# A static schedule rebuilt on measured ScalarE constants, and a GpSimd normalisation placed in halves beside VectorE's PSUM reads

## The chip, the cores and the metric

The kernel runs on one core of one Trainium2 chip. The metric is the device time of one execution in microseconds (us), median of several. The profiled execution of each kernel is one of those; its span, from first to last instruction, is about 2 us shorter than its time.

## The reference, cut to what matters

```python
x  = A_x                                   # 2048 tokens of 512, bf16
xn = layernorm(x)
# 32 heads of width 16; the scores are 32 x 2048 x 2048
o  = softmax(q @ k.T * 0.25) @ v           # q, k, v from xn @ wqkv
return x + o @ wo + (silu(xn @ w1) * (xn @ w3)) @ w2      # hidden width 1792
```

The exponentials are the bulk: 1024 tiles of 128x1024 scores. Most go through ScalarE's table; the rest are built on VectorE from integer operations on the bits of bf16 numbers.

Of the kernel before, what the change touches and what calls it, by code (L numbers as in the profile page):

```python
# [142 lines left out]

_LAT = 0.06
_LATS = {("pe", "act"): 0.041, ("pe", "dve"): 0.053, ("dve", "pool"): 0.083, ("pool", "dve"): 0.033, ("act", "dve"): 0.033}
_TAILS = {"act": 0.182, "dve": 0.083, "pool": 0.05, "sp": 0.0}


class _Sched(_Prog):
# [25 lines left out]
    def _time(self, op, deps, dur, tail, mode=None, rows=None):  # L175
        ready = self._ready(op, deps)
        if op.eng != "pe":
            start = max(self.free[op.eng], ready)
            op.end = start + dur + tail
            self.free[op.eng] = start + dur  # L180
            return op
        lm, lr, ls = self.pem
        if mode == "row":
            if lm == "row":
                gap = 0.217 if rows & lr else 0.007
            else:
                gap = 0.318
            start = max(ready, ls + gap)
            self.pem = (mode, rows | lr if gap < 0.1 and start < ls + 0.2 else rows, start)
            self.free["pe"] = start + 0.01  # L190
        elif mode == "col":
            start = max(ready, ls + (0.217 if lm == "col" else 0.318))
            self.pem = (mode, frozenset(), start)
            self.free["pe"] = start + 0.2
        else:
            start = max(ready, ls + (0.217 if lm == "x" else 0.318))
            self.pem = (mode, frozenset(), start + dur - 0.217)
            self.free["pe"] = start + dur
        op.end = start + dur + tail
        return op  # L200
# [836 lines left out]
def _plan_fast(nc, ps, flag, A_x, A_wqkv, A_wo, B_w1, B_w3, B_w2, out):  # L1037
# [49 lines left out]
    with ctx:  # L1087
# [65 lines left out]
        def xk(s0, n):  # L1153
            return [("xnT", t) for t in range(s0 // 128, (s0 + n) // 128)]

        a_cost = lambda n: 0.049 + 0.000834 * n
        d_cost = lambda n: 0.054 + 0.00106 * n
        s_cost = lambda n: 0.075 + 0.000261 * n

# [416 lines left out]
        def tile_OUT(tg, part):  # L1576
            qc, ts = divmod(tg, 4)

            def og(g, slot, key):
                return (lambda i: onorm[:, slot, ts * 128 + 32 * i:ts * 128 + 32 * i + 32], wo[:, g, :],  # L1580
                        [("ON", slot), ("wor", g)],
                        lambda: have(key))
            ffn = [(lambda i, fc=fc: hT[:, fc, ts * 128 + 32 * i:ts * 128 + 32 * i + 32], w2[:, fc, :],
                    [("hT", fc), ("w2", fc)], None) for fc in range(FC)]
# [61 lines left out]
            return _T("O%d_%d" % (tg, part), groups, evac, cond=cond, start=None if part in (2, 4) else start)  # L1646


        st = {"dbl": 0, "pos": 0, "pv": 0, "dbal": 0, "nd": 0, "lastA": -1.0, "n_exp": 0, "wait_a": 0, "hold_d": 0, "last_par": 0}
        pbuf = [0.0] * 3  # L1650
        pr_free = [0.0] * NPR
        yfree = [0.0] * NY
# [222 lines left out]
        def try_d():  # L1875
            if st["pos"] >= NR or st["early"] or st["hold_d"] or not d_due():
                return False
            free = open_bufs()
            if not free or (len(free) == 1 and st["wait_a"] == 0):
                return False  # L1880
            nx = d_next()
            buf = free[-1]
            b0 = 2 * buf
            x = score(b0, "D", *nx) if nx is not None else None
            if x is None:
                return False
            st["hold_d"] = 1
            u, j0, kt, o = x
            st["dbal"] += 1 - j0
            nd_unit[u] += 1  # L1890
            for i in range(2):
                ndj[u][j0 + i] += 1
            pbuf[buf] = 1e9
            sl = dcur[0]
            if sl is None:
                sl = dcur[0] = {"y": None, "p1": 0, "n": 0, "ch": [], "done": 0, "max": 2 if u < NU - 1 or left[u] > D_ONE else 1}
            c = sl["n"]
            sl["n"] += 1
            last = sl["n"] == sl["max"]
            if last:  # L1900
                dcur[0] = None
            sl["ch"].append((u, j0, kt))

            def p1():
                if sl["y"] is None:
                    sl["y"] = free_slot(yfree)
                    yfree[sl["y"]] = 1e9
                ys = sl["y"]
                q = P.op("dve", lambda e: e.tensor_scalar(dsl[:, ys, 1024 * c:1024 * c + 1024], ps[:, b0 * 512:b0 * 512 + 1024],  # L1909
                                                          YB, G_LO, ALU.add, ALU.max),  # L1910
                         reads=[("ps", b0), ("ps", b0 + 1)], writes=[("ds", ys, 2 * c), ("ds", ys, 2 * c + 1)] + xd_keys(ys, 1024 * c, 1024 * c + 1024), dur=d_cost(1024), name="p1")
                pbuf[buf] = q.end + _LAT
                st["hold_d"] = 0
                sl["p1"] += 1
                if last:
                    chain(sl)
            prev = dprev[0] if c == 0 else sl["prev"]
            if c == 0:
                sl["prev"] = prev
                dprev[0] = sl  # L1920
            need = 1 if c == 0 else 2
            P.post("dve", p1, ready=o.end + _LAT, prio=2,
                   cond=lambda: (sl["y"] is not None or free_slot(yfree) is not None) and
                   (prev is None or prev["done"] >= need))
            return True
# [113 lines left out]
        def unit_end(u, o):  # L2039
# [33 lines left out]
            def e4():  # L2073
# [3 lines left out]
                        reads=[("Rrow",)], writes=[("R", j, h)], kb=32)  # L2077
                if h or u == NU - 2:
                    eng = "dve" if u == NU - 2 else "pool"
                    P.post(eng, lambda: e5(eng), ready=q.end + _LAT, prio=0, cond=lambda: u // 2 < NON or all(  # L2080
                        ("OUT", (u // 2 - NON) // NP * 4 + i) in done for i in range(4)))

            def e5(eng):
                on = (u // 2) % NON
                if u == NU - 2:
                    q = P.op(eng, lambda e: e.scalar_tensor_tensor(onorm[:, on, :], U[:, 0, :], msk[:, 0:1], R[:, :],
                                                                   ALU.mult, ALU.mult),
                             reads=[("Uc",), ("msk", 0)] + [("R", j_, h_) for j_ in range(4) for h_ in range(2)],
                             writes=[("ON", on)], dur=0.68)
                    done[("ON", qc, pi)] = q.end + _LAT  # L2090
                    return
                q = P.op(eng, lambda e: e.tensor_tensor(onorm[:, on, :], U[:, 0, :], R[:, :], ALU.mult),  # L2092
                         reads=[("Uc",)] + [("Uo", j_) for j_ in range(4)] +
                         [("R", j_, h_) for j_ in range(4) for h_ in range(2)], writes=[("ON", on)],
                         dur=0.6 if eng == "dve" else 1.3)
                done[("ON", qc, pi)] = q.end + _LAT
                done[("e5", u // 2)] = q.end
            if u == NU - 1:
                return last_end(o)
            P.post("dve", e0, ready=o.end + _LAT, prio=0, cond=lambda: u < 2 or h == 1 or ("e5", u // 2 - 1) in done)  # L2100
# [1 line left out]
        def last_end(o):  # L2102
# [36 lines left out]
            def norm_b():  # L2139
                q = P.op("dve", lambda e: e.scalar_tensor_tensor(onorm[:, ON_B, :], U[:, 1, :], msk[:, 1:2], bank(PV),  # L2140
                                                                 ALU.mult, ALU.mult),
                         reads=[("Ut",), ("ps", PV), ("msk", 1)], writes=[("ON", ON_B)], dur=0.597)
                done[("ON", qc, "B")] = q.end + _LAT
            P.post("act", copy, ready=o.end + _LAT, prio=0)

# [205 lines left out]
```

## The kernel before: what the change touches

The program contains a scheduler. It runs before launch, keeps a clock of its own, decides greedily which operation comes next on every engine, and emits each engine's instruction list in that order. On the chip the lists are fixed, and semaphores alone connect them. A constant such as `a_cost` (ScalarE, n columns) or one of `_TAILS` (from end of issue to result) is therefore no instruction: it changes only what the scheduler believes, and so the order.

```python
_TAILS = {"act": 0.182, "dve": 0.083, "pool": 0.05, "sp": 0.0}   # from end of issue to result
...
# _Sched._time: TensorE, switching between score matmuls ("row") and others ("col")
            if lm == "row":
                gap = 0.217 if rows & lr else 0.007
            else:
                gap = 0.318
...
        elif mode == "col":
            start = max(ready, ls + (0.217 if lm == "col" else 0.318))
...
    def dma(...):                       # a landing as the scheduler reckons it
        self._time(op, op.deps, 0.56, 0.0)
        self.ring = max(self.ring, op.end) + kb / rate
        op.end = self.ring + 1.5
...
        a_cost = lambda n: 0.049 + 0.000834 * n      # ScalarE, n columns
        d_cost = lambda n: 0.054 + 0.00106 * n       # VectorE from PSUM
```

Who takes the next tile of scores follows from the engines' believed states: a tile goes to VectorE whenever it is nearly free, else to ScalarE. A VectorE tile costs a PSUM read (`p1`, 1024 columns) and four operations per two tiles from SBUF to SBUF: two masks and an add (L1951, L1967, L1973) and a product (L1958).

Every second unit (a unit is four heads by 512 queries, 32 in all) ends with a normalisation. Row sums are inverted, sent through DMA so that each spreads over its 16 partitions (`R`), and GpSimd multiplies:

```python
            def e4():
                for j in range(4):
                    q = P.dma(lambda e, j=j: e.dma_start(
                        R[32 * j + 16 * h:32 * j + 16 * h + 16, :], Rrow[j:j + 1, :]...broadcast_to([1, 16, 512])), ...)
                if h or u == NU - 2:
                    eng = "dve" if u == NU - 2 else "pool"
                    P.post(eng, lambda: e5(eng), ready=q.end + _LAT, prio=0, cond=...)

            def e5(eng):                # 128x512 fp32 times fp32 -> bf16; 15 times on GpSimd
                q = P.op(eng, lambda e: e.tensor_tensor(onorm[:, on, :], U[:, 0, :], R[:, :], ALU.mult), ...)
```

## Time and profile before

| | before |
|---|---|
| time, median of 3 | 801.17 us |
| ScalarE, share of the span | 97% (801 exponentials, 56 tanh, 19 others) |
| VectorE | 96% (223 tiles of exponentials and all else) |
| TensorE | 94%, not a measure of its peak |
| GpSimd | 4% |

Three engines are busy nearly all the time, so shares tell little. ScalarE's *work* is the sum of its back-to-back intervals between the first and the last exponential (0.9165 us for an exponential, 0.490 us for a tanh). Its *lost time* is what the stretch between the ends of those two takes beyond the work. Work, lost time, what precedes the end of the first exponential and what follows the end of the last add up to the span. Before: 764.5 + 7.3 + 13.0 + 13.6 = 798.4 us. I worked this out from the records of the trace, and split the lost time into three stretches: to 110 us, 110 to 770 us, and from 770 us on.

### The profile page before, as it was taken

The page shows a single profiled execution, that of the slowest core. Times are in us where ns is not written, and L with a number is a line of the kernel's source. Part 1 is how long each engine was busy: PE and PEld are TensorE (multiplying, and loading weights), DVE is VectorE, ACT ScalarE, POOL GpSimd, SP SyncE. Part 2 cuts the span into 40 slices and gives each one's busy share as a digit, 9 for nine tenths or more (in the row PEclk, how much of TensorE's full clock was granted, in tenths as well). Part 3 has the DMA queues.
Part 4 walks back from the last instruction along what each step waited for, and adds up shares of the span by engine and source line. Part 5 has one row for each costly group of instructions (what it writes and reads, how often), then busy time and mean ns, then how long its engine had stood idle before and what let it go on. Part 6 is the DMA issues. An engine that isn't in the chain of part 4 may idle for free.

```text
span 798.4 us, 21147 instructions
## 1 busy us (share of the span) xinstructions
PE 754.4 (94%) x9157; PEld 222.4 (28%) x9157; DVE 766.3 (96%) x1032; ACT 774.9 (97%) x876; POOL 32.8 (4%) x45
## 2 busy tenths in 40 slices
PE   8998999999999999999999999999999989999996
PEld 6322322222222222222222222222222222222222
DVE  8898999999999999999999999999999999999984
ACT  6999999999999999999999999999999999999993
POOL 3100100000000000000000000000000000000000
PEclk9999999999999999999999999999999999999998
DMA  6032233332222233133221233322223341332211
GB/s 212 2 60 68 16 42 35 43 44 24 48 37 29 28 46 50 31 46 55 36 21 30 34 48 43 54 28 50 21 22 41 49 55 19 52 34 23 29 8 33
DMA packets 83727, 32.91 MB, mean 41 GB/s; under 512 B 72104, under 2 KB 80040, under 8 KB 83624
## 3 DMA queue, kind: packets, MB, share of 16 engines
q1 hardware_dynamic: 83624, 31.46, 27.5%
q8 instruction: 74, 1.21, 0.6%
q14 instruction: 29, 0.24, 0.1%
HBM read 22.81 MB, written 2.10 MB: 31 GB/s over the span
## 4 chain that ended last, share of the span: by engine, by line
ACT 65%; DVE 18%; PE 14%; issue 1%; DMA 1%; POOL 0%; SPq 0%; DVEq 0%
ACT f_PT L1837 62%; DVE f_xd L1909 5%; PE ps L1328 5%; PE ps L1774 4%; PE ps L2027 4%; DVE f_xd L1958 3%; ACT f_th L1542 3%; DVE f_xd L1951 2%; DVE f_xd L1973 1%; DVE f_xd L1967 1%; DVE f_t L1546 1%; DVE f_hT L1556 1%; DVE f_stats L1252 1%; DMA f_R<-f_Rrow 1%; DVE f_U L2045 0%
## 5 line engine op out<-in xcount | busy, mean ns | idle before, releaser
L1837 ACT ACTIVATE f_PT<-ps 128x1024 bf16<-128x1024 f32 x801 | 751.7, 1155 | 4.8 <-PE ps L1774 2.7
L1774 PE MATMUL ps<-f_QT,f_KT 32*128 32x512 bf16 x2048 | 313.4, 385 | 25.8 <-ACT f_PT L1837 17.8
L1909 DVE TENSOR_SCALAR f_xd<-ps 128x1024 int16<-128x1024 f32 x223 | 271.5, 1218 | 4.8 <-PE ps L1774 3.5
L2027 PE MATMUL ps<-f_PT,f_Vaug 128*17 128x512 bf16 (+1 forms) x1602 | 211.7, 385 | 1.0 <-DVE f_U L2045 0.4
L2027 PE MATMUL ps<-f_xd,f_Vaug 128*17 128x512 bf16 (+1 forms) x1338 | 185.8, 385 | 4.3 <-DVE f_U L2045 1.8
L1774 PEld LDWEIGHTS ps<-f_QT,f_KT 32*128 32x128 bf16 x2048 | 78.8, 91 | 332.7 <-ACT f_PT L1837 272.1
L1328 PE MATMUL ps<-f_xnT,f_w 128*32 128x512 bf16 x1792 | 140.6, 384 | 3.9 <-DVE f_t L1546 3.2
L1958 DVE TENSOR_TENSOR f_xd<-f_xd 128x2048 bf16<-128x2048 bf16 x112 | 138.2, 1234 | 0.0
L1951 DVE TENSOR_SCALAR f_xd<-f_xd 128x2048 int16<-128x2048 int16 x112 | 78.2, 698 | 2.2 <-PE ps L2027 1.6
L1973 DVE TENSOR_SCALAR f_xd<-f_xd 128x2048 int16<-128x2048 int16 x112 | 80.1, 715 | 0.0
L1967 DVE TENSOR_SCALAR f_xd<-f_xd 128x2048 int16<-128x2048 int16 x112 | 76.5, 683 | 0.0
L1328 PE MATMUL ps<-f_w,f_hT 128*32 128x512 bf16 x896 | 75.5, 384 | 0.0
L2027 PEld LDWEIGHTS ps<-f_PT,f_Vaug 128*17 128x17 bf16 (+1 forms) x1602 | 50.8, 92 | 58.5 <-issue 45.6
L2027 PEld LDWEIGHTS ps<-f_xd,f_Vaug 128*17 128x17 bf16 (+1 forms) x1338 | 44.7, 92 | 50.0 <-issue 26.9
L1328 PEld LDWEIGHTS ps<-f_xnT,f_w 128*32 128x32 bf16 x1792 | 36.1, 94 | 62.6 <-issue 52.5
L2092 POOL TENSOR_TENSOR f_onorm<-f_U,f_R 128x512 bf16<-128x512 f32 x15 | 22.2, 1482 | 710.3 <-DMA f_R<-f_Rrow 616.8
L1542 ACT ACTIVATE f_th<-ps 128x512 f32<-128x512 f32 x56 | 41.4, 739 | 0.0
L1546 DVE SCALAR_TENSOR_TENSOR f_t<-f_th,ps 128x512 bf16<-128x512 f32 x56 | 38.1, 681 | 1.8 <-ACT f_th L1542 1.3
L1556 DVE SCALAR_TENSOR_TENSOR f_hT<-f_t,ps 128x512 bf16<-128x512 bf16 x56 | 38.1, 680 | 0.8 <-PE ps L1328 0.6
L1328 PEld LDWEIGHTS ps<-f_w,f_hT 128*32 128x32 bf16 x896 | 17.9, 94 | 25.5 <-issue 21.1
L1328 PE MATMUL ps<-f_wo,f_onorm 128*32 128x512 bf16 x272 | 21.6, 387 | 0.8 <-DVE f_wkv L1599 0.4
L2045 DVE COPY f_U<-ps 128x512 f32<-128x512 f32 x31 | 21.3, 686 | 0.0
(82 smaller groups left out, 239.8 us busy)
## 6 DMA issues: line engine op xcount, KB each, us to landing
f_w<-in_B_w_dram SPq DMA_DIRECT2D x112, 128.0 KB, 2.4
f_R<-f_Rrow SPq DMA_DIRECT2D x124, 32.0 KB, 4.0
f_xr<-in_A_x_dram SPq DMA_DIRECT2D x16, 128.0 KB
out_dram<-f_xn_sb SPq DMA_DIRECT2D x16, 128.0 KB
f_U<-f_U SPq DMA_DIRECT2D x60, 32.0 KB, 2.0
f_w<-in_B_w_dram SPq DMA_DIRECT2D x7, 256.0 KB
f_xd<-in_A_x_dram SPq DMA_DIRECT2D x3, 512.0 KB
f_xd<-in_A_x_dram SPq DMA_DIRECT2D x2, 256.0 KB
```

The costliest lines, as they stand in the source:

```text
L1328: ins = e.matmul(bank(bk)[32 * i:32 * i + 32, 0:ncols], make_lhsT(i), rhs_ap, start=start, stop=stop, tile_position=(0, 32 * i))
L1542: q = P.op("act", lambda e: e.activation(th[:, ss, :], bank(bk), ACTF.Tanh, scale=0.5), reads=[("ps", bk)], writes=[("th", ss)], dur=a_cos ...
L1546: q2 = P.op("dve", lambda e: e.scalar_tensor_tensor(t1[:, ss, :], th[:, ss, :], 1.0, bank(bk), ALU.add, ALU.mult), reads=[("th", ss), ("ps ...
L1556: q = P.op("dve", lambda e: e.scalar_tensor_tensor(hT[:, fc, :], t1[:, ss, :], 0.5, bank(bk), ALU.mult, ALU.mult), reads=[("t1", ss), ("ps ...
L1774: ins = e.matmul(bank(b), l_, r_, start=True, stop=True, tile_position=(rp, 0))
L1837: q = P.op("act", lambda e: e.activation(PT[:, s_, :], ps[:, b0 * 512:(b0 + 2) * 512], ACTF.Exp, scale=ASC, bias=ABIAS), reads=[("ps", b0) ...
L1909: q = P.op("dve", lambda e: e.tensor_scalar(dsl[:, ys, 1024 * c:1024 * c + 1024], ps[:, b0 * 512:b0 * 512 + 1024], YB, G_LO, ALU.add, ALU. ...
L1951: P.op("dve", lambda e: e.tensor_scalar(dsl[:, NY + m_, 0:n], y, 0x7F, 0x3F00, ALU.bitwise_and, ALU.bitwise_or), reads=YK, writes=[("ds", ...
L1958: q_ = P.op("dve", lambda e: e.tensor_tensor(t_ap.bitcast(BF16), y.bitcast(BF16), t_ap.bitcast(BF16), ALU.mult), reads=YK + [("ds", NY + m ...
L1967: q_ = P.op("dve", lambda e: e.tensor_scalar(g_ap, y, -G_LO, 0.0, ALU.add, ALU.max), reads=YK, writes=[("g", g_, k) for k in range(n // 51 ...
L1973: q_ = P.op("dve", lambda e: e.tensor_scalar(y, y, 0x7F80, None, ALU.bitwise_and), reads=YK, writes=YK, dur=s_cost(n), name="e", lock=True)
L2027: ins = e.matmul(bank(PV)[32 * j:32 * j + (17 if g % 2 == 0 else 32), :], v_, p_, start=s0, stop=s1, tile_position=(0, 32 * j))
```

## The change

Its intent is twofold: let the scheduler plan with ScalarE's real rate, so that the two exponential engines are loaded in the right proportion; and split each GpSimd normalisation into two halves that run while VectorE reads PSUM. In the trace before, the 10 PSUM reads beside such a GpSimd operation took at most 1.23 us, as the others did; only steps from SBUF to SBUF were stretched there.

```diff
-_TAILS = {"act": 0.182, ...
+_TAILS = {"act": 0.105, ...
-                gap = 0.318
+                gap = 0.325
-            start = max(ready, ls + (0.217 if lm == "col" else 0.318))
+            start = max(ready, ls + (0.219 if lm == "col" else 0.32))
-        a_cost = lambda n: 0.049 + 0.000834 * n
+        a_cost = lambda n: 0.0615 + 0.000834 * n
@@ p1: the PSUM read of a VectorE tile
+                st["p1_at"], st["p1_op"] = P.t, P.ops["dve"][-1]      # the operation before it
@@ unit_end
-                    P.post(eng, lambda: e5(eng), ready=q.end + _LAT, ...)
+                    P.post(eng, (lambda: e5(eng)) if eng == "dve" else (lambda: e5h(0)), ready=q.end + _LAT, prio=0,
+                           cond=lambda: (eng == "dve" or beside_p1()) and (...))
+            def beside_p1():
+                return st["p1_at"] == P.t
+            def e5h(i):
+                cs = slice(256 * i, 256 * i + 256)
+                q = P.op("pool", lambda e: e.tensor_tensor(onorm[:, on, cs], U[:, 0, cs], R[:, cs], ALU.mult),
+                         ..., writes=[("ON", on, i)], dur=0.72, extra=[st["p1_op"]])
+                if i == 0:
+                    P.post("pool", lambda: e5h(1), ready=q.end + _LAT, prio=0, cond=beside_p1)
+                    return
```

More of the change, by code (lines that the diff above doesn't have):

```diff
@@ L145 @@
 _LATS = {("pe", "act"): 0.041, ("pe", "dve"): 0.053, ("dve", "pool"): 0.083, ("pool", "dve"): 0.033, ("act", "dve"): 0.033}
-_TAILS = {"act": 0.182, "dve": 0.083, "pool": 0.05, "sp": 0.0}
+_TAILS = {"act": 0.105, "dve": 0.083, "pool": 0.05, "sp": 0.0}
 class _Sched(_Prog):
@@ L1580, in og @@
                 return (lambda i: onorm[:, slot, ts * 128 + 32 * i:ts * 128 + 32 * i + 32], wo[:, g, :],
-                        [("ON", slot), ("wor", g)],
+                        [("ON", slot, ts // 2), ("wor", g)],
                         lambda: have(key))
@@ L1646, in tile_OUT @@
             return _T("O%d_%d" % (tg, part), groups, evac, cond=cond, start=None if part in (2, 4) else start)
-        st = {"dbl": 0, "pos": 0, "pv": 0, "dbal": 0, "nd": 0, "lastA": -1.0, "n_exp": 0, "wait_a": 0, "hold_d": 0, "last_par": 0}
+        st = {"dbl": 0, "pos": 0, "pv": 0, "dbal": 0, "nd": 0, "lastA": -1.0, "n_exp": 0, "wait_a": 0, "hold_d": 0, "last_par": 0, "p1_at": -1.0, "p1_op": None}
         pbuf = [0.0] * 3
@@ L2079, in e4 @@
                     eng = "dve" if u == NU - 2 else "pool"
-                    P.post(eng, lambda: e5(eng), ready=q.end + _LAT, prio=0, cond=lambda: u // 2 < NON or all(
-                        ("OUT", (u // 2 - NON) // NP * 4 + i) in done for i in range(4)))
+                    P.post(eng, (lambda: e5(eng)) if eng == "dve" else (lambda: e5h(0)), ready=q.end + _LAT, prio=0, cond=lambda: (eng == "dve" or beside_p1()) and (u // 2 < NON or all(
+                        ("OUT", (u // 2 - NON) // NP * 4 + i) in done for i in range(4))))
@@ new lines, in beside_p1 @@
+            def beside_p1():
+                return st["p1_at"] == P.t
+            def e5h(i):
+                on = (u // 2) % NON
+                cs = slice(256 * i, 256 * i + 256)
+                q = P.op("pool", lambda e: e.tensor_tensor(onorm[:, on, cs], U[:, 0, cs], R[:, cs], ALU.mult),
+                         reads=[("Uc",)] + [("Uo", j_) for j_ in range(4)] +
+                         [("R", j_, h_) for j_ in range(4) for h_ in range(2)], writes=[("ON", on, i)], dur=0.72,
+                         extra=[st["p1_op"]])
+                if i == 0:
+                    P.post("pool", lambda: e5h(1), ready=q.end + _LAT, prio=0, cond=beside_p1)
+                    return
+                done[("ON", qc, pi)] = q.end + _LAT
+                done[("e5", u // 2)] = q.end
@@ L2083, in e5 @@
             def e5(eng):
                 on = (u // 2) % NON
-                if u == NU - 2:
-                    q = P.op(eng, lambda e: e.scalar_tensor_tensor(onorm[:, on, :], U[:, 0, :], msk[:, 0:1], R[:, :],
-                                                                   ALU.mult, ALU.mult),
-                             reads=[("Uc",), ("msk", 0)] + [("R", j_, h_) for j_ in range(4) for h_ in range(2)],
-                             writes=[("ON", on)], dur=0.68)
-                    done[("ON", qc, pi)] = q.end + _LAT
-                    return
@@ L2092, in e5 @@
-                q = P.op(eng, lambda e: e.tensor_tensor(onorm[:, on, :], U[:, 0, :], R[:, :], ALU.mult),
-                         reads=[("Uc",)] + [("Uo", j_) for j_ in range(4)] +
-                         [("R", j_, h_) for j_ in range(4) for h_ in range(2)], writes=[("ON", on)],
-                         dur=0.6 if eng == "dve" else 1.3)
+                q = P.op(eng, lambda e: e.scalar_tensor_tensor(onorm[:, on, :], U[:, 0, :], msk[:, 0:1], R[:, :],
+                                                               ALU.mult, ALU.mult),
+                         reads=[("Uc",), ("msk", 0)] + [("R", j_, h_) for j_ in range(4) for h_ in range(2)],
+                         writes=[("ON", on, 0), ("ON", on, 1)], dur=0.68)
@@ L2096, in e5 @@
                 done[("ON", qc, pi)] = q.end + _LAT
-                done[("e5", u // 2)] = q.end
             if u == NU - 1:
@@ L2141, in norm_b @@
                                                                  ALU.mult, ALU.mult),
-                         reads=[("Ut",), ("ps", PV), ("msk", 1)], writes=[("ON", ON_B)], dur=0.597)
+                         reads=[("Ut",), ("ps", PV), ("msk", 1)], writes=[("ON", ON_B, 0), ("ON", ON_B, 1)], dur=0.597)
                 done[("ON", qc, "B")] = q.end + _LAT
```

## The prediction

> **What bounds the kernel now.** The order of every engine's instructions is made before launch by a greedy scheduler inside the program, which keeps its own clock from duration constants. The change edits those constants and one GpSimd step, so I asked first which engines are saturated, then where the scheduler's constants differ from the trace, then what the GpSimd step does to its neighbours.
>
> The page of the kernel before, engines and chain:
> ```profile
> PE 754.4 (94%) x9157; PEld 222.4 (28%) x9157; DVE 766.3 (96%) x1032; ACT 774.9 (97%) x876; POOL 32.8 (4%) x45
> ...
> ACT 65%; DVE 18%; PE 14%; issue 1%; DMA 1%; POOL 0%; SPq 0%; DVEq 0%
> ```
> ScalarE leads, with VectorE beside it. They share one job: 1024 exponentials of 128x1024 scores, 801 on ScalarE, 223 on VectorE. The stretch of 40 to 780 us, where this work runs:
> ```profile
> 40.00:780.00 740.00, 705.78 (x8346) 196.00 (x8338) 725.53 (x936) 737.83 (x830) 23.34 (x19) 1.00 0.28 38
> ```
> ScalarE is idle 2.2 us of 740 here, VectorE 14.5 us, TensorE (whose busy time I don't trust as a peak) 34 us. So each exponential fewer on ScalarE, and each gap in it, moves the end; VectorE has idle room. The last 18 us are another stage (final units, output), which the change barely touches.
>
> ScalarE's real rate, from the groups, the records of that line and the chain of waits:
> ```profile
> L1837 ACT ACTIVATE f_PT<-ps 128x1024 bf16<-128x1024 f32 x801 | 751.7, 1155 | 4.8 <-PE ps L1774 2.7
> L1837 ACT ACTIVATE f_PT<-ps x801: 1017/1168/1348, 11.9 to 783.8; 128x1024 bf16<-128x1024 f32 x161
> 28.47 78.87 ACT f_PT L1837 x86
> 237.65 49.63 ACT f_PT L1837 x54
> ```
> Queued records overlap, so the mean of 1155 is no rate. From ends of successive exponentials I get a median of 0.917 us (710 of 739 intervals under 0.93, mean 0.9166). An unqueued one takes 1.017. The scheduler before believes 0.049 + 0.000834*1024 = 0.903 and an end at 0.903 + 0.182 = 1.085. So it thinks ScalarE 1.5% too fast and its results 0.07 us too late. A 512-wide tanh takes 0.490 from end to end, believed 0.476. The VectorE constants are right: PSUM read 1.139 believed, 1.134 measured; 16-bit steps 0.610 against 0.601; product 1.133 against 1.133.
>
> The error explains VectorE's idle time: 801 x (0.9166 - 0.903) + 56 x 0.014 = 11.7 us by which real ScalarE falls behind the plan; everything coupled to it slips with it, and VectorE idles 14.5 us. It was handed too little.
>
> GpSimd's 15 normalisations, one near 466 us on VectorE, GpSimd and ScalarE, then one near 132 us:
> ```profile
> 466.22 2.30 DVE L1958 TENSOR_TENSOR f_xd<-f_xd 128x2048 bf16<-128x2048 bf16 x1
> ...
> 466.09 1.35 POOL L2092 TENSOR_TENSOR f_onorm<-f_U,f_R 128x512 bf16<-128x512 f32 x1 [43.92 <-DMA f_R<-f_Rrow]
> ...
> 470.48 8.36 ACT L1837 ACTIVATE f_PT<-ps 128x1024 bf16<-128x1024 f32 x9 [0.61 <-PE ps L2027]
> ...
> 132.00 1.23 DVE L1909 TENSOR_SCALAR f_xd<-ps 128x1024 int16<-128x1024 f32 x1
> 133.14 0.68 DVE L1437 CAST f_KT<-ps 128x512 bf16<-128x512 f32 x1
> ...
> 132.53 1.27 POOL L2092 TENSOR_TENSOR f_onorm<-f_U,f_R 128x512 bf16<-128x512 f32 x1 [38.58 <-DMA f_R<-f_Rrow]
> ```
> At 466 the product, usually 1.22, takes 2.30, and ScalarE runs dry two microseconds after it. At 132 the GpSimd operation lies beside two PSUM reads and neither is longer than usual.
>
> **What the Trainium skill says.** "SBUF — State Buffer", section "SBUF: two separate sides": the port pair that VectorE shares with GpSimd is an exclusive lock; a VectorE operation in a 2-port mode, or with two SBUF inputs, and a GpSimd operation block each other for a whole instruction. The trace agrees: ten SBUF-to-SBUF operations were stretched by 0.04 to 1.08 us, no PSUM read was. "GPSIMD Engine Reference", section 3.1, gives 4497 ns for a two-input add of 2048 fp32 elements; with the 1.271 us undisturbed minimum here for 512, an estimate: 2.10 ns an element and 0.196 us fixed, so half costs 0.73 us. "ScalarE: Activation LUTs", section "What ACT_TABLE_LOAD costs", gives 0.833 ns an element, and 93 ns of overlap back to back; the slope of the constant agrees, and 1.017 - 0.9166 gives 0.100 us of overlap.
>
> **The change part by part.**
>
> 1. *ScalarE rate 0.903 to 0.9155, tail 0.182 to 0.105.* Interval now right (0.9155 against 0.9166), end too (1.0205 against 1.017). The plan gives VectorE a bigger share. If d exponentials move, one pair costs VectorE 1.134 + (3 x 0.601 + 1.133)/2 = 2.602 us and frees 0.9155 in the plan. Both engines stay full in the plan: 857 x 0.0125 = 10.7 us more planned ScalarE time must spread, so 2.602 d = 10.7 - 0.9155 d, d = 3.0. I expect 798 on ScalarE and 226 on VectorE. In real time ScalarE loses 3 x 0.9166 = 2.8 us. VectorE gains 7.8 us, which fits its idle time. TensorE gets for each moved pair four more value products, one group of 0.217 us: 0.65 us, hidden in its 34.
>
> 2. *GpSimd halves beside PSUM reads.* Each half is issued with a dependence on the VectorE operation just before a 128x1024 PSUM read. The trace has 0.05 to 0.11 us from a VectorE release to a GpSimd start; plus 0.73 that ends 0.85 us into a read of 1.13. It fits with 0.28 to spare. Removed: VectorE stretches, from each record less its median: three products 0.45 + 1.08 + 0.86; five adds/masks of L1973 1.08 + 1.08 + 0.89 + 0.39 + 0.04; two of L1951 1.08 + 0.48; sum 7.4 us. On the path is only what reaches ScalarE: end-to-end intervals over 0.916 in the few microseconds after those hits sum to 0.65 (near 230), 0.45 (327), 0.55 (425), 0.78 (470), 0.67 (520), 0.48 (614): 3.6 us, of 4.0 in all until 780. I take 3.6. The normalised result comes about 3 to 5 us later, since two reads, on average 740/223 = 3.3 us apart, must be met. The next normalisation is some 45 us away; consumers waited for this tile 0.7 us in all, so this costs nothing.
>
> 3. *TensorE switch gaps 0.318 to 0.325 and 0.320, column groups 0.217 to 0.219.* Measured medians: column to row 0.322, row to column 0.318, column to column 0.216 to 0.228. It only makes the plan honest; I count 0.
>
> Against this: so far real ScalarE was behind its plan, which swallowed whatever planned idleness ScalarE had. An honest plan shows it. Measured idle time outside the GpSimd hits is only 0.45 us; I take back 1.2 us.
>
> Sum: -2.8 - 3.6 + 1.2 = -5.2 us, so 796.0 from 801.2.
>
> **The rivals.**
>
> *VectorE becomes the bound.* If d is 6 or more, it adds 15.6 us against 14.5 idle plus 7.4 of stretches: it just fits, and the chain would show VectorE growing. The ceiling is both engines without a gap: 0.917 d + 4 = 22 - 2.6 d, d = 5.1, gain 8.7 us: 792.5. For it: the constants are now true. Against: gaps of VectorE such as 1.9 us at 65 and 1.25 at 410, where it waits for TensorE, are holes of the schedule that remain.
>
> *TensorE order takes over.* A shorter tail issues scores about 0.065 us earlier, and larger gaps hold more room for TensorE. If its 34 us idle are mostly in the wrong places, ScalarE waits for scores and the gain is 0 to 3 us: 798 to 801. For it: 0.79 us holes before rows at the 99th percentile of gaps. Against: of ScalarE's 4.8 us waits in the line above, nearly all follow GpSimd hits or lie in the tail.
>
> *The greedy order is chaotic.* Any constant reshuffles it; early phase and tail may move by 1 to 2 us each. The tail holds a wait of 4.3 us for TensorE. That could give 793 or 800 without a mechanism.
>
> *GpSimd hits survive.* If its start after the release is late by over 0.28 us, the next 16-bit step is still hit, twice as often: 30 halves at up to 0.5 us. Gain of part 2 gone: about 799.6.
>
> **Range and chances.** Ceiling 8.7 us plus 2 of luck gives about 790.5 at the low end; no gain with slight bad luck 800.5 at the high end. Over 2% (16 us) is beyond every sum here: 0.02. Slower by 2% would take a broken order, as a normalisation that never meets its read: 0.02.
>
> **What would show it.** Right: exponentials at 797 to 800, 30 GpSimd halves of about 0.73 us, the largest L1951, L1973 and L1958 records near their medians (0.69, 0.69, 1.22) instead of 1.77 to 2.30; VectorE idle in the same stretch under 10 us; exponential intervals still 0.917. Wrong: ScalarE idle in that stretch above 5 us (planned idleness shown), a count of 801 or more, or a tail over 20 us.

## The result, and the profile after

Ratios here and below are the mean time of one kernel's fast runs over that of the other's fast runs of the same rounds, so not quite the ratio of the medians quoted.

| | time, median | ratio to before, 95% interval |
|---|---|---|
| after, in a job of its own before the experiments (4 runs) | 800.27 us (before: 800.89) | 0.9994 (0.9976 to 1.0011) |
| after, again in the third job of experiments (e9, 6 runs) | 799.72 us (before: 801.04) | 0.9979 (0.9967 to 0.9991) |

The gain is 0.5 to 1.7 us, not 5.2. The page of the changed kernel, engines, chain and the two groups (from `p1` on, its lines stand one lower than before: L1910 is the PSUM read that was L1909, L1952, L1959, L1968 and L1974 are the steps that were L1951, L1958, L1967 and L1973):

```profile
PE 749.9 (94%) x9169; PEld 227.4 (28%) x9169; DVE 768.3 (96%) x1039; ACT 772.7 (97%) x873; POOL 39.0 (5%) x60
...
ACT 60%; DVE 25%; PE 11%; issue 2%; DMA 1%; SPq 0%; POOL 0%; DVEq 0%; ACTq 0%
...
L1837 ACT ACTIVATE f_PT<-ps 128x1024 bf16<-128x1024 f32 x798 | 747.9, 1141 | 6.7 <-PE ps L1774 3.9
...
L2090 POOL TENSOR_TENSOR f_onorm<-f_U,f_R 128x256 bf16<-128x256 f32 x30 | 26.1, 874 | 702.9 <-DMA f_R<-f_Rrow 411.0
```

798 exponentials, as worked out beforehand. But ScalarE's idle time before them grew from 4.8 to 6.7 us, and the chain moved from ScalarE towards VectorE (18% to 25%). The halves average 874 ns where 730 would be undisturbed. The busy times of 40 to 780 us (columns: stretch, length, then TensorE, weight loads, VectorE, ScalarE, GpSimd, granted clock, DMA share, GB/s):

```profile
40.00:780.00 740.00, 702.85 (x8380) 201.51 (x8376) 729.39 (x948) 735.15 (x827) 29.69 (x34) 1.00 0.28 38
```

ScalarE is idle 4.9 us here, against 2.2 before; VectorE 10.6 against 14.5. The account of ScalarE for both:

| us | work | lost to 110 | 110 to 770 | from 770 | before first end + after last | span |
|---|---|---|---|---|---|---|
| before | 764.5 | 1.6 | 4.1 | 1.7 | 26.5 | 798.4 |
| after | 761.8 | 3.4 | 3.7 | 2.3 | 26.8 | 798.0 |

The work fell by 2.7 us. The middle, where 3.6 us should have gone, lost 0.4 less. The other two stretches gave back 2.5 us.

Two places show how. First ScalarE near 68 us: a gap which the kernel before, whose ScalarE ran through this stretch, does not have. It waits for scores; the projection of the next unit's queries stands just ahead of them on TensorE.

```profile
65.36 2.17 ACT L1837 ACTIVATE f_PT<-ps 128x1024 bf16<-128x1024 f32 x2
68.83 1.94 ACT L1837 ACTIVATE f_PT<-ps 128x1024 bf16<-128x1024 f32 x2 [1.30 <-PE ps L1774]
```

Second, the halves: what ended GpSimd's wait before each, in the view of that line (columns: releaser, idle us in total, times).

```profile
L2090 POOL TENSOR_TENSOR f_onorm<-f_U,f_R x30: 723/730/2096, 82.1 to 759.3; 128x256 bf16<-128x256 f32 x30
its engine sat idle before it (us, times) until:
  DMA f_R<-f_Rrow: 411.0, 9
```

By this view, nine of the 15 first halves were not released by the VectorE operation that they were to follow, but by the landing of `R`, which came after it. The view undercounts. VectorE's semaphore is updated at the end of every VectorE operation, and the view names whichever update came last. By the update times in the trace, four more first halves start 0.16 us after the last landing, as the nine do (one at 229.98 us, last landing at 229.82), while a half that VectorE does release starts about 0.07 us after it. So it was 13 of 15, and all six stretches of VectorE in this profile lie at halves of these 13 normalisations. The timelines of VectorE, GpSimd and ScalarE at one of these (start, duration, engine, operation):

```profile
562.43 1.22 DVE L1959 TENSOR_TENSOR f_xd<-f_xd 128x2048 bf16<-128x2048 bf16 x1
563.57 1.22 DVE L1952 TENSOR_SCALAR f_xd<-f_xd 128x2048 int16<-128x2048 int16 x1
564.71 1.21 DVE L1974 TENSOR_SCALAR f_xd<-f_xd 128x2048 int16<-128x2048 int16 x1
...
562.96 2.41 POOL L2090 TENSOR_TENSOR f_onorm<-f_U,f_R 128x256 bf16<-128x256 f32 x2 [48.98 <-DMA f_R<-f_Rrow]
...
564.41 2.09 ACT L1837 ACTIVATE f_PT<-ps 128x1024 bf16<-128x1024 f32 x2
566.74 4.21 ACT L1837 ACTIVATE f_PT<-ps 128x1024 bf16<-128x1024 f32 x4 [0.24 <-PE ps L1774]
```

`R` landed during the product at 562.43, when the PSUM read meant for the first half was over. GpSimd waited for the product, then held up the next two 16-bit steps: 1.22 us each instead of 0.69. Two microseconds later ScalarE had no scores.

I call the excess of a SBUF-to-SBUF VectorE record over the median of its line a *hit*. There are ten hits of 7.4 us in sum before, and six of 2.8 us after.

### The profile page after: what moved, and what is told of

The parts are those of the page before. It is cut to its first block, busy times and chain, and to the rows that moved or that the text cites. A ratio compares the mean times of both kernels' runs of the same rounds, so it can differ in the third digit from the quotient of the medians.

```text
span 798.0 us, 21199 instructions
## 1 busy us (share of the span) xinstructions
PE 749.9 (94%) x9169; PEld 227.4 (28%) x9169; DVE 768.3 (96%) x1039; ACT 772.7 (97%) x873; POOL 39.0 (5%) x60
## 4 chain that ended last, share of the span: by engine, by line
ACT 60%; DVE 25%; PE 11%; issue 2%; DMA 1%; SPq 0%; POOL 0%; DVEq 0%; ACTq 0%
ACT f_PT L1837 57%; DVE f_xd L1910 8%; PE ps L1328 4%; DVE f_xd L1959 4%; PE ps L1774 4%; DVE f_xd L1952 3%; PE ps L2028 2%; DVE f_xd L1968 2%; ACT f_th L1542 2%; DVE f_xd L1974 2%; DVE f_hT L1556 2%; DVE f_t L1546 1%; DVE f_U L2046 1%; DMA f_R<-f_Rrow 1%; DVE f_QT L1456 0%
## 5 line engine op out<-in xcount | busy, mean ns | idle before, releaser
L1774 PE MATMUL ps<-f_QT,f_KT 32*128 32x512 bf16 x2048 | 310.0, 386 | 26.4 <-ACT f_PT L1837 20.2
L1910 DVE TENSOR_SCALAR f_xd<-ps 128x1024 int16<-128x1024 f32 x226 | 275.1, 1217 | 3.7 <-PE ps L1774 3.5
L2028 PE MATMUL ps<-f_PT,f_Vaug 128*17 128x512 bf16 (+1 forms) x1596 | 209.0, 385 | 3.4 <-DVE f_U L2046 2.1
L2028 PE MATMUL ps<-f_xd,f_Vaug 128*32 128x512 bf16 (+1 forms) x1356 | 181.7, 384 | 6.4 <-DVE f_xd L1974 3.7
L1959 DVE TENSOR_TENSOR f_xd<-f_xd 128x2048 bf16<-128x2048 bf16 x113 | 137.3, 1215 | 0.0
L1952 DVE TENSOR_SCALAR f_xd<-f_xd 128x2048 int16<-128x2048 int16 x113 | 79.9, 707 | 2.8 <-PE ps L2028 1.9
L1974 DVE TENSOR_SCALAR f_xd<-f_xd 128x2048 int16<-128x2048 int16 x113 | 78.0, 691 | 0.0
L1968 DVE TENSOR_SCALAR f_xd<-f_xd 128x2048 int16<-128x2048 int16 x113 | 77.5, 686 | 0.0
L1328 PE MATMUL ps<-f_w,f_hT 128*32 128x512 bf16 x896 | 72.6, 383 | 0.2
L2090 POOL TENSOR_TENSOR f_onorm<-f_U,f_R 128x256 bf16<-128x256 f32 x30 | 26.1, 874 | 702.9 <-DMA f_R<-f_Rrow 411.0
L2028 PEld LDWEIGHTS ps<-f_xd,f_Vaug 128*32 128x32 bf16 (+1 forms) x1356 | 44.9, 93 | 54.3 <-issue 26.9
```

The source lines that it names most:

```text
L1328: ins = e.matmul(bank(bk)[32 * i:32 * i + 32, 0:ncols], make_lhsT(i), rhs_ap, start=start, stop=stop, tile_position=(0, 32 * i))
L1774: ins = e.matmul(bank(b), l_, r_, start=True, stop=True, tile_position=(rp, 0))
L1910: q = P.op("dve", lambda e: e.tensor_scalar(dsl[:, ys, 1024 * c:1024 * c + 1024], ps[:, b0 * 512:b0 * 512 + 1024], YB, G_LO, ALU.add, ALU. ...
L1952: P.op("dve", lambda e: e.tensor_scalar(dsl[:, NY + m_, 0:n], y, 0x7F, 0x3F00, ALU.bitwise_and, ALU.bitwise_or), reads=YK, writes=[("ds", ...
L1959: q_ = P.op("dve", lambda e: e.tensor_tensor(t_ap.bitcast(BF16), y.bitcast(BF16), t_ap.bitcast(BF16), ALU.mult), reads=YK + [("ds", NY + m ...
L1968: q_ = P.op("dve", lambda e: e.tensor_scalar(g_ap, y, -G_LO, 0.0, ALU.add, ALU.max), reads=YK, writes=[("g", g_, k) for k in range(n // 51 ...
```

## The experiments

**What the scheduler's own clock says.** The scheduler is part of the program, so its plan can be read without a chip. It is no measurement; it says what an order contains if all its constants were true.

```
                          end    exp. ScalarE/VectorE   planned ScalarE gaps over 1 us, 40 to 770 us
before                   780.0         801 / 223        none
constants alone (e1)     790.4         799 / 225        1.48 at 68
halves alone (e2)        780.7         802 / 222        none
after                    788.7         798 / 226        1.48 at 68
halves, later R (e6)     781.5         801 / 223        none
halves + rate (e7)       791.3         799 / 225        1.46 at 69, 1.15 at 81
halves + tail (e12)      785.6         800 / 224        4.76 at 70
e8                       786.8         797 / 227        none
```

The order after has a gap of 1.48 us near 68 us in its own plan. The order before has none, but its planned end of 780 us was not met: the chip took 798 us for it.

Results of all runs (exponentials on ScalarE; us; the hits' sum is of VectorE from 40 us on):

| run | time | ratio (95%) | exp. | work | lost to 110 / middle / from 770 | rest | span | hits |
|---|---|---|---|---|---|---|---|---|
| e1 constants alone | 802.55 | 1.0019 (1.0005 to 1.0032) | 799 | 762.7 | 3.6 / 3.4 / 1.6 | 27.6 | 798.9 | 4.0 |
| e2 halves alone | 796.28 | 0.9940 (0.9928 to 0.9952) | 802 | 765.5 | 1.6 / 0.5 / 0.4 | 26.4 | 794.3 | 2.2 |
| e3 before, 32 columns | 796.89 | 0.9951 (0.9938 to 0.9964) | 801 | 764.6 | 1.5 / 0.3 / 1.8 | 26.7 | 794.8 | 0.3 |
| e4 after, 32 columns | 797.15 | 0.9948 (0.9935 to 0.9961) | 798 | 761.8 | 3.7 / 0.3 / 2.7 | 26.4 | 794.9 | 0.2 |
| e5 after, later R | 797.16 | 0.9944 (0.9931 to 0.9957) | 798 | 761.8 | 3.4 / 0.3 / 2.9 | 26.8 | 795.1 | 0 |
| e6 halves, later R | 797.89 | 0.9949 (0.9936 to 0.9962) | 801 | 764.5 | 1.5 / 1.5 / 0.0 | 28.7 | 796.2 | 0 |
| e7 halves + rate | 802.58 | 1.0010 (0.9997 to 1.0022) | 799 | 761.2 | 4.9 / 2.6 / 2.2 | 30.4 | 801.2 | 1.5 |
| e8 e5 + other order | 795.30 | 0.9928 (0.9914 to 0.9942) | 797 | 760.9 | 1.9 / 0.4 / 2.1 | 27.2 | 792.3 | 1.0 |
| e9 after again | 799.72 | 0.9979 (0.9967 to 0.9991) | 798 | 761.8 | 3.4 / 3.2 / 2.9 | 26.8 | 798.1 | 4.0 |
| e10 e6, hits on purpose | 801.02 | 0.9999 (0.9986 to 1.0011) | 801 | 764.5 | 2.4 / 4.1 / 0.0 | 29.1 | 800.1 | 8.4 |
| e11 e5, hits on purpose | 801.67 | 1.0004 (0.9991 to 1.0017) | 798 | 761.8 | 3.9 / 5.6 / 2.1 | 26.7 | 800.2 | 5.6 |
| e12 halves + tail | 807.92 | 1.0092 (1.0068 to 1.0116) | 800 | 764.1 | 5.5 / 0.8 / 1.5 | 30.5 | 802.4 | 1.3 |

e1 to e4 ran in one job, e5 to e8 in a second, e9 to e12 in a third, each job on another chip; times compare best within a job. The columns of work, lost time, rest, span and hits are of one profiled execution, which need not be the median one. e3 and e4 give wrong results; all others were correct.

### e1: the constants alone

```diff
 # the kernel before, with
+_TAILS = {"act": 0.105, ...;  gap = 0.325;  0.219 / 0.32;  a_cost 0.0615 + ...
```

> The kernel before with the constants of the change alone; the GpSimd normalisation stays whole and unplaced. In the scheduler's own clock this order has 799 exponentials on ScalarE and 225 on VectorE, and one planned ScalarE gap of 1.48 us near 68 us that the order before does not have. I call lost time what lies between the ends of ScalarE's first and last exponential over the sum of its back-to-back intervals (before 7.3 us, after 9.4). Theory (the change removes ScalarE work, and gives it back in a planned gap near 68 us and in GpSimd hits that survive): two exponentials fewer save 1.8, the gap costs 1.4, hits stay as before at about 3.6 us on ScalarE and 5 to 8 us on VectorE: 799.5 to 801.5 us, lost time 8 to 10. Rival (the constants are a pure gain of 2.8 us or more, the halves lose it again): 797 to 798.5, lost time 7 or less.

Measured: lost time 8.7 us, as expected, but a median of 802.55 us, 1 us above the expectation's top. The profile does not explain that: it is of the fastest of the six executions (800.70 us, within the range). In it the stage after the last exponential took 1.0 us more than before, which the expectation had not counted; what made the other five longer is not shown. The constants are no gain by themselves: this order has the gap near 68 us, too. The rival falls.

### e2: the halves alone

```diff
 # the changed kernel, with the constants of before
+_TAILS = {"act": 0.182, ...;  gap = 0.318;  0.217 / 0.318;  a_cost 0.049 + ...
```

> The change without its constants: only the two GpSimd halves beside PSUM reads. The scheduler's clock gives 802 exponentials on ScalarE and 222 on VectorE (one more than before). Theory: one exponential more costs 0.9, most of the 3.6 us of hits go, some 1 to 2 us survive where the landing of f_R comes after the read that the half was placed beside: 798.5 to 800.5 us, lost time 4.5 to 6.5, VectorE stretches over 0.2 us from 7.4 down to 1 to 3 us in sum. Rival (hits were absorbed elsewhere and never cost time): 801 to 802.5, lost time 7 or more.

Measured: 796.28 us, better than my theory. Hits fell as expected (2.2 us), but they cost ScalarE only 0.5 us between 110 and 770 us. **One part of the change alone beats the whole by 0.4 to 0.5%.** A caveat: 1.3 us of the 4.9 us that its lost time is below before's lie after 770 us. There the profile of before has a half-clock interval (a stretch in which TensorE's granted clock is 0.5) at 780 us, and this one has none; see the last section.

### e3 and e4: the contention taken away, the order kept

```diff
-   onorm[:, slot, ts * 128 + 32 * i:ts * 128 + 32 * i + 32]          # read by the output matmuls
+   onorm[:, slot, 0:32]                                               # e4: from column 256 on for the second half
-   e.tensor_tensor(onorm[:, on, :], U[:, 0, :], R[:, :], ALU.mult)
+   e.tensor_tensor(onorm[:, on, 0:32], U[:, 0, 0:32], R[:, 0:32], ALU.mult)
```

> The kernel before, same order on every engine, but the GpSimd normalisation works on 32 of the 512 columns (and the output matmuls read those 32 columns again and again, in the same shapes): a wrong result on purpose, which takes the contention away and nothing else. GpSimd operations take 0.25 to 0.35 us. Theory (hits reach ScalarE with 3.6 us): lost time 7.3 to between 3.5 and 4.5 us, 797 to 798 us. Rival (ScalarE would have waited anyway a little later): lost time 6 or more, 800 to 801 us.

Measured e3: lost time 7.3 to 3.6 us, of it 4.1 to 0.3 in the middle, time 4.6 us less. The instruction order was the same on TensorE, VectorE, ScalarE and the DMA queue. So 3.8 us of ScalarE's time is what the ten hits cost the kernel before, and the prediction's 3.6 was right as a size. The place near 466 us again, ScalarE and then VectorE and GpSimd:

```profile
466.82 9.30 ACT L1837 ACTIVATE f_PT<-ps 128x1024 bf16<-128x1024 f32 x10
...
464.22 1.28 DVE L1958 TENSOR_TENSOR f_xd<-f_xd 128x2048 bf16<-128x2048 bf16 x1
...
464.00 0.41 POOL L2092 TENSOR_TENSOR f_onorm<-f_U,f_R 128x32 bf16<-128x32 f32 x1 [44.34 <-DMA f_R<-f_Rrow]
```

The product takes 1.28 instead of 2.30 us, and ScalarE runs through ten exponentials where it had stopped for 0.61 us.

> The changed kernel with halves of 32 columns each, same order, wrong result on purpose. Theory (five surviving hits of 2.45 us in sum on VectorE, about 1.7 us of lost time on ScalarE): lost time 9.4 to between 7 and 8.3 us, 798 to 799 us; the gap near 68 us of 1.4 us and what lies near 315 us stay. Rival (the surviving hits cost nothing, the new lost time is all order): 800 to 800.7 us, lost time above 9.

Measured e4: lost time 6.7 us, below the range, and 797.15 us, 1 us better than expected. The surviving hits cost more than I had put on them: the middle fell from 3.7 to 0.3 us. One part of that, 1.1 us near 315 us, is no hit but a half-clock interval that this run did not have there. The gap near 68 us stayed.

### e5: the first half placed by a later landing

```diff
-   ... (lambda: e5h(0)), ready=q.end + _LAT, prio=0
+   ... (lambda: e5h(0)), ready=q.end + _LAT + (0 if eng == "dve" else 2.0), prio=0
```

> The changed kernel, in which the scheduler takes the landing of f_R 2.0 us later before it places the first GpSimd half; every other engine's order is unchanged (the scheduler's clock says 788.7 us with and without). Section 6 of the page has 4.1 us from issue to landing of f_R, the scheduler reckons about 2.2. Theory (the six surviving hits, 2.8 us in sum on VectorE, come from halves that were released by the DMA after their PSUM read had begun, and reach ScalarE with about 2 us): hits near 0, ScalarE's lost time from 9.4 to 6.2 to 7.5 us, 797.2 to 798.7 us. Rival (they cost nothing): lost time above 9, 800 us.

Measured: no hits at all, middle 3.7 to 0.3 us (1.1 of the 3.7 lay around the half-clock interval near 315 us), 797.16 us: 4.4 us below before in its job, while the changed kernel itself is 0.5 to 1.7 us below. As each engine's list is the same as in the changed kernel, only semaphore waits of GpSimd differ. The view of the halves, then the timeline of GpSimd and ScalarE near the same place:

```profile
L2090 POOL TENSOR_TENSOR f_onorm<-f_U,f_R x30: 723/728/737, 82.9 to 757.6; 128x256 bf16<-128x256 f32 x30
its engine sat idle before it (us, times) until:
...
  DMA f_R<-f_Rrow: 124.9, 3
```

```profile
563.67 0.73 POOL L2090 TENSOR_TENSOR f_onorm<-f_U,f_R 128x256 bf16<-128x256 f32 x1 [48.69 <-DVE f_t L1546]
...
562.56 13.08 ACT L1837 ACTIVATE f_PT<-ps 128x1024 bf16<-128x1024 f32 x14
```

The longest half takes 737 ns, not 2096; VectorE releases it, and ScalarE does 14 exponentials without a stop. Why 2.0 us nearly suffice is in the DMA part of the page of the changed kernel: 4.1 us from issue to landing of `R` at the median (3.4 to 4.6 in the six records that have a landing), where the scheduler reckons 0.56 + 32/270 + 1.5 = 2.2. A few landings still come late (three halves by this view, four by the update times), but each of these halves still fell beside a PSUM read, and no step was stretched.

### e6: the halves alone with the later landing

```diff
 # e2, with the + 2.0 of e5
```

> The halves alone (the faster of the two parts), with the same later landing. The scheduler gives 801 and 223. Theory: its seven hits (2.2 us on VectorE, 0.4 us of ScalarE's lost time between 110 and 770 us) go, one exponential fewer saves 0.9: 795 to 796.2 us, lost time 2 to 3. Rival (the placing of halves is luck): 796.3 or more.

Measured: hits gone, but 797.89 us, above the expectation and within noise of e2's ratio (0.9949 against 0.9940). The orders of ScalarE and VectorE changed with it (801 and 223, as against 802 and 222), so it isn't e2 with the hits removed and nothing else. Of its 1.5 us in the middle, 1.4 lie around a half-clock interval at 358 us, and 2.0 us came on after the last exponential. e2's hits had cost next to nothing, so taking them away won nothing. Note also that e5, which has the constants besides, has practically the same ratio (0.9944): with the hits out of the way, the constants neither gain nor lose measurably.

### e7 and e12: one constant at a time on the halves

```diff
 # e7: e2, with a_cost 0.0615 + 0.000834 * n        # e12: e2, with "act": 0.105
```

> The halves with the ScalarE rate of the change, but the old tail of 0.182 and the old TensorE gaps. The scheduler gives 799 and 225, and plans two ScalarE gaps of 1.46 us near 69 and 1.15 us near 81 us. Theory (the honest rate saves work and gives it back in gaps that the order contains and that a too fast rate had hidden): against the halves alone, 3 exponentials fewer save 2.75, planned gaps cost about 2.6 plus 0.5 in the first 40 us, surviving hits 1 to 2: 797 to 798.5 us, lost time 6.5 to 8. Rival (the tail or the TensorE gaps do the harm, not the rate): 793.5 to 795.5 us, lost time under 4.

Measured e7: 802.58 us, 6.3 us above e2. Its work is 4.3 us less (2.7 of it are three exponentials; the rest are three small copies before 40 us that VectorE does in this order). It loses 3.3 us more in the first 110 us, where the two planned gaps show as 1.3 and 0.9 us; 2.1 more in the middle (1.1 of it at a half-clock interval near 690 us); 1.8 more from 770 us on; and 3.7 more after the last exponential. My theory had the first two terms and missed the last two.

> The halves with the shorter ScalarE tail alone; old rate and gaps. The scheduler gives 800 and 224 and plans one ScalarE gap of 4.76 us near 70 us. Theory (planned gaps are real, less what ScalarE lags its plan since the last gap: by 70 us about 60 exponentials x 0.0135 = 0.8 us): 3.5 to 4.3 us lost there, 2 exponentials fewer save 1.8, so 1.5 to 3 us above the halves alone: 797.8 to 799.5 us. Rival (the shorter tail by itself is good): 794 to 796 us and no gap above 1 us.

Measured e12: ScalarE in the stretch concerned:

```profile
71.62 1.94 ACT L1837 ACTIVATE f_PT<-ps 128x1024 bf16<-128x1024 f32 x2 [4.41 <-PE ps L1774]
```

Lost time there is 4.5 us for a planned gap of 4.76: a planned gap is paid nearly in full, so the lag of ScalarE behind a too fast plan hides little. The time was missed by 8 us, and it spreads widely (804.3 to 810.9). In the profile, which is of the fastest execution, 3.7 us more than in e2 lie after the last exponential (17.2 instead of 13.6 us). The five slower executions have no profile; their granted clocks are lower (0.987 to 0.997, against 1.000). Neither the rate nor the tail is harmless alone, and each harms through the gaps and the end of the order that the greedy scheduler falls into. The TensorE gaps alone were not run.

### e8: the changed kernel, later landing, another order

```diff
 # e5, with
-    PVQ = 28;  VBS = 5
+    PVQ = 24;  VBS = 6
```

> The changed kernel with the later landing and two knobs of the order (value tiles at every 6th instead of every 5th position, value products begun from a backlog of 24 instead of 28), chosen because the scheduler's clock then has no gap near 68 us: 797 and 227. Theory: hits gone and the gap gone: work 0.9 less and lost time 4.5 to 6 us, 795 to 796.5 us. Rival (another order brings other gaps): 797.5 or more.

Measured: 795.30 us, the lowest of all, as expected: 0.7% below before (its interval overlaps those of e5 and e2). Not all hits are gone, though: five of 1.0 us in sum stayed. The gap near 68 us is gone (1.9 us lost to 110 us instead of 3.4), the middle loses 0.4 us.

### e9: the changed kernel again

> The changed kernel as it is, once more, for a comparison on one chip with the other runs. All theories: 0 to 1.5 us below the kernel before (ratio 0.998 to 1.0), hits six of 2.8 us in sum on VectorE, ScalarE's lost time 8.5 to 10. If it were 3 us or more below, the later landing (4 us below before) would have won little.

Measured: 799.72 us, as expected. Nine hits of 4.0 us this time, six of them of the same normalisations as in the first profile; the middle lost 3.2 us with no half-clock interval in it. So the loss is there without the clock: 2.9 us above e5 from 4.0 us of hits here, and 2.3 us from 2.8 us in the first profile, if the 1.1 us near 315 us are taken off.

### e10 and e11: hits on purpose in two orders

```diff
 # e6 and e5; the scheduler's plan is left as it is, then the half is made to wait for the read itself
+                q.deps.append(st["p1_self"])          # the PSUM read, not the operation before it
```

> The order of the halves with later landing (old constants), unchanged on every engine, but each GpSimd half waits for the PSUM read itself instead of for the operation before it, so that it falls beside the next operation: hits on purpose, at 10 to 20 of 30 halves, 0.4 to 0.6 us each. Theory of slack (with the too fast ScalarE rate VectorE is given less, idles 16 us between 40 and 780 us and catches up, so that a hit costs ScalarE under 40% of its length): hits 6 to 10 us in sum, ScalarE's lost time between 110 and 770 us up by 1 to 3.5 us, 797 to 800.5 us. Rival (a hit costs ScalarE the same in every order, 80% and more): up by 5 to 8 us, 802 or more.

> The same hits on purpose in the order of the changed kernel with later landing (its lost time between 110 and 770 us was 0.3 us, its VectorE idle time 9.8 us). Theory of slack: over 70% of the hits' sum of 6 to 10 us reach ScalarE: lost time in that stretch 4.5 to 8 us, 801.5 to 805 us. Rival: the same share of the hits as in the run beside it.

| | hits | lost time up, to 770 us | share |
|---|---|---|---|
| e10 (order of old constants), against e6 | 8.4 us, 17 hits | 3.5 us | 42% |
| e11 (order of new constants), against e5 | 5.6 us, 16 hits | 4.5 us | 80% |

(For e11, 1.3 us around a half-clock interval near 316 us are left out, as e5 has none in the middle; e10 and e6 both have one. Between 110 and 770 us alone, the stretch of the expectations, e10 loses 2.6 us more than e6 for 7.8 us of hits, and e11 loses 4.0 us more than e5 for 4.9.) The same split is in the runs that were not made for it: before against e3, 3.8 of 7.1 us (54%); e2, at most 0.5 of 2.2; after again against e5, 2.9 of 4.0 us (72%); e1, at most 3.4 of 4.0. So a hit costs more in the second order than in the first. The theory of slack would explain it: where ScalarE is planned too fast, VectorE gets less and can swallow a part of a hit. The idle time of VectorE between 40 and 780 us, as the sum of the gaps before its operations there, is 16.6 us in e6 and 9.8 us in e5. But that slack, and not another trait of those orders, is the cause is not shown: no run changed the slack alone, and e1 speaks against it. There VectorE idles 15.0 us in the same stretch, as long as before (14.5), and yet up to 3.4 of 4.0 us of hits seem to have reached ScalarE. e11's time of 801.67 us lies at the lower end of its expectation, e10's slightly above its own.

One theory fell on the way. I first thought that a too fast ScalarE plan keeps more finished scores waiting in front of ScalarE. The time from the end of a tile's score matmuls to the start of its exponential's record, worked out by matching each exponential to the matmuls that it depends on, has a median of 0.17 us before and 0.18 us after, so there is no such difference.

## Why the prediction was wrong

- **What bounds the kernel**: right. ScalarE's work and gaps set the end in every run, and the account adds up to the span.
- **Part 1, the split**: right to the instruction (798 and 226), -2.7 us of work against -2.8.
- **The reason given for VectorE's idle time**: only partly right. It was laid to ScalarE's lag behind its plan, so an honest plan should have filled it. In the stretch it fell from 14.5 to 10.6 us only; the scheduler's own plan holds 10 us of VectorE idle time in both orders. The ceiling of 8.7 us was built on this and was too high in its VectorE term.
- **Part 2, the step that failed**: "It fits with 0.28 to spare." That sum had the right duration (0.73 us, measured 0.730) and the right release latency, but the wrong releaser. It took VectorE as what releases a half. Most first halves (nine by the view, 13 of 15 by the update times) were released by the landing of `R`, planned 2 us too early, when their PSUM read was under way or over. The page before had the 4.0 us to landing and the code the 2.2, and the prediction did not compare them. Of the 3.6 us, which e3 shows to be about the true size (3.8), 0.4 arrived in the first profile and 0.9 in e9's; e5 got the rest with that one delay (0.3 us lost in the middle, against 3.7 and 3.2 in the two profiles of the changed kernel).
- **The rival "GpSimd hits survive"** named the outcome (about 799.6) with another cause, a slow start after VectorE's release.
- **The 1.2 us for planned idleness**: right in kind, too small: 1.8 us more lost before 110 us, of it 1.4 in the gap near 68 us that the plan itself holds (1.48 there), and 0.7 more from 770 us on.
- **Sum**: -2.7 of work, -0.4 in the middle, +1.8 and +0.7 at the two ends, +0.2 before the first exponential: -0.4 us, the difference of the two spans.
- **Its own signs of being right or wrong**: the count (798) came true. The halves (mean 874 ns instead of about 730), the largest SBUF-to-SBUF steps (1.22 us instead of 0.69) and VectorE's idle time (10.6 us, not under 10) did not; ScalarE's idle time of 4.9 us stayed just under the 5 us that would have shown planned idleness.
- What was not foreseen at all: that the same hits cost more in the new order (80% of a hit in e11, 42% in e10). Why stays open, as said there.

## What to carry to other kernels

When an operation is placed beside another, list everything that can release it, and compare the planned time of each with the measured one; the latest decides, and it was a DMA. A recalibrated static schedule should be judged by its order, gaps of its own plan included, and by each part alone: here the halves alone were worth 4 to 5 us, and with the constants on top most of that was gone. With the hits removed (e5) the two together were worth as much as the halves alone (e6). So take the disturbances out before judging new constants: the same disturbance cost more in the order that they made.

## What the Trainium skill lacked or had wrong

- "SBUF — State Buffer", section "SBUF: two separate sides": the exclusive port pair is confirmed (VectorE's PSUM reads keep 1.22 us beside a GpSimd half; 16-bit steps go from 0.69 to 1.22 us). What it lacks is that a GpSimd operation can wait behind a chain of such VectorE operations, and not only behind one: a half of 0.73 us was recorded with up to 2.10 us (in the changed kernel at 130.87 us, through three 16-bit steps in a row).
- "ScalarE: Activation LUTs", section "What ACT_TABLE_LOAD costs": its two formulas give 1.039 us (immediate scale and bias) and 1.133 us (pointer bias) for 1024 columns as estimates; unqueued exponentials from PSUM took 1.017 us here. The overlap of 93 ns agrees (1.017 - 0.9166 = 0.100).
- "TensorE: Matmul & The Clock Gate", section "What's actually happening", has the clock halved after an idle window of about 3.4 us (further down, the same page tells of a kernel whose short idle times between groups of matmuls were enough). Here half-clock intervals of 3.41 us fall into the middle of a busy kernel. Those at 312 us (after), 358 us (e6), 362 us (e10), 688 us (e7) and 314 us (e11) each follow a 3.41 us window in which TensorE was busy for 2.2 to 2.4 us, so it was far from idle. Other windows as low (2.1 us at 380 us in before) had no such consequence. What decides stays open. The same stretch of the changed kernel and of e5, with the granted clock in the third column from the right:

```profile
310.00:320.00 10.00, 9.69 (x106) 2.34 (x108) 8.99 (x13) 9.10 (x11) 0.00 (x0) 0.83 0.45 51
```

```profile
310.00:320.00 10.00, 9.67 (x122) 2.73 (x122) 10.00 (x14) 10.00 (x13) 0.00 (x0) 1.00 0.47 53
```

  Same order, 0.9 us of ScalarE's time. In e9, the changed kernel again, no such interval falls here and no time is lost near 316 us. No page says what such an interval costs a kernel that three engines share: here 1.0 to 1.4 us were lost around each in the middle (0.97 us of it in one interval between exponentials in the changed kernel). Runs of one kernel that differ by up to 3 us differ in the granted clock too (e8: 794.4 us at 0.999, 797.4 at 0.995).
- No page has the landing time of a small broadcast DMA from SBUF to SBUF (4.1 us at the median from issue for 32 KB, four in a row on one queue), nor the time of a two-input GpSimd operation this small (fp32 multiply to bf16: 0.73 us at 256 columns, 1.27 at 512, undisturbed).
